# Two-layer product behind a windowed attention: the second layer's stationary tiles are moved by 128 bytes

## The chip, the cores and the metric

The kernel runs on one core of a Trainium2 chip. The metric is the device time of one execution in microseconds, median of the runs shown. The profile is one further execution, seen by the hardware profiler, and its span runs from the first to the last instruction.

## What is computed

An attention over 8 batches, 8 heads, 576 positions and 64 values a head, in which each query sees 32 keys (the last 32 for the first four heads, every fourth of the last 128 for the others), gives 4608 rows of 512 numbers. A two-layer product follows:

```python
h = x @ w_in                       # 4608x512 by 512x2048
g = where(h >= 1, h, where(h <= -1, 0, (h + 1)**2 / 4))
out = g @ w_out                    # 4608x2048 by 2048x512
```

All of it is float32. The weights' words are rebuilt in the kernel from 64-bit input.

## The kernel before

The 4608 rows are cut into 9 tiles of 512 (`TOK`), the 2048 middle columns into 16 chunks of 128 (`NF`), which makes 144 steps (t, f). Each float32 operand of the two layers is split into a high and a low part of type fp32r (`gh` and `gl`, `xh` and `xl`, and two parts of each weight), and a product is the sum of three: high by high, low by high, high by low.

A step of the first layer (`layer1`, L412) is 12 matmuls into one PSUM bank: the stationary operand is a 128x128 block of `wi`, the moving one 128x512 of `xh` or `xl`. The activation of the step follows on VectorE and ScalarE: clamp into a tile `y` (L422), square (L428), maximum with h (L432), high part into `gh` (L439), low part into `gl` (L444). A step of the second layer is again 12 matmuls (L458), with a 128x128 block of `gh` or `gl` stationary and 128x512 of `wo` moving, into four banks that collect over the 16 chunks of a tile:

```python
terms = ((gh, 0), (gl, 0), (gh, 1))
for m, i in order or [(m, i) for m in range(TOK // 128) for i in range(3)]:
    g, w = terms[i]
    PE.matmul(
        out=acc[m],
        lhsT=g[:, 128 * m : 128 * m + 128],
        rhs=weight("wo", f, w, slice(0, DM)),
```

Each matmul is a pair of instructions on TensorE: the load of the stationary block (LDWEIGHTS, PEld in the profile) and the matmul proper. Each second-layer and first-layer matmul has its own load.

The first tile's work is written out by hand in a string of step names (`FIRST`), with the attention of the first eight head pairs and the unpacking of the weights between. From the second tile on a loop sets TensorE's order: `layer1` of step s, then for some steps the scores (L162) or the values (L306) of a later head pair, then `layer2` of step s - 2. So the second layer uses `gh` and `gl` two steps after the first layer has given their h, and in every second step or so some 70 short matmul instructions of the scores or 24 of the values stand between `layer1` and `layer2`. In the last part (from about 705 us) only the two layers are left.

All tiles of SBUF lie in two pools, one after the other along each partition, one place for each tag in the order in which the tags are first asked for. Bytes of a place in each partition, in that order: `small` 2944, `pts` 4608, `qk` 4736, then `wi6`, `wo6`, `wi7`, three buffers of `xh`, `wo7`, three of `xl` (8192 each), `v` 6144, `wi0`, `wi1`, `wo0` (8192), two of `c` (3328), `m0` 4096, `wi2` 8192, `m1` 4096, `wo1`, `wi3`, `wo2`, `wi4`, `wo3`, `wi5`, `wo4` (8192 each), `y` 2048, `gh0`, `gl0`, `gh1`, `gl1`, `gh2`, `gl2` (2048 each), and last `wo5` 8192. The three `gh` and three `gl` places are taken in turn by the steps. Every place after `qk` is a multiple of 256 bytes, so all of `wi`, `wo`, `xh`, `xl`, `y`, `gh` and `gl` start at the same address modulo 256; the places end 384 bytes below the end of the 224 KiB of a partition.

Of the kernel before, what the change touches and what calls it, by code (L numbers as in the profile page):

```python
# [6 lines left out]
F32 = mybir.dt.float32  # L7
F32R = mybir.dt.float32r
# [13 lines left out]
TOK = 512  # L22
NT = B * S // TOK
NF = DF // 128
# [39 lines left out]
def body(ctx, tc, qk, v, v2, mask, w_in, w_out, out):  # L64
# [4 lines left out]
    pool = ctx.enter_context(tc.tile_pool(name="pool", bufs=1))  # L69
# [331 lines left out]
    gs, hps, acc, outs = {}, {}, {}, {}  # L401
# [16 lines left out]
            )  # L418

    def clamped(t, f):  # L420
        gs[t, f] = [pool.tile([128, TOK], F32, tag="y", name=f"y{t}_{f}")]
        nc.vector.tensor_scalar(  # L422
            out=gs[t, f][0], in0=hps[t, f], scalar1=-1.0, scalar2=1.0, op0=ALU.max, op1=ALU.min
        )
# [7 lines left out]
        done.append([nc.vector.tensor_tensor(out=hp, in0=hp, in1=gs[t, f][0], op=ALU.max)])  # L432

    def g_tile(tag, t, f):
        gs[t, f].append(pool.tile([128, TOK], F32R, tag=f"{tag}{(t * NF + f) % 3}", name=f"{tag}{t}_{f}"))
        return gs[t, f][-1]

    def g_high(t, f):
        done[-1].insert(0, nc.scalar.copy(out=g_tile("gh", t, f), in_=hps[t, f]))  # L439

    def g_low(t, f):
        hp = hps.pop((t, f))
        gh = gs[t, f][1]
        nc.vector.tensor_tensor(out=g_tile("gl", t, f), in0=hp, in1=gh.bitcast(F32), op=ALU.subtract)  # L444

    def activation(t, f):
        with tc.high_priority(offset=60):
            for part in (clamped, squared, larger, g_high, g_low):
                part(t, f)
# [83 lines left out]
    def constants_step(count, where):  # L533
# [15 lines left out]
        "E": lambda _, name: block(low_part)(name),  # L549
        "h": products1, "o": products2,  # L550
        "clamp": chunk(clamped), "sq": chunk(squared), "mx": chunk(larger), "gh": chunk(g_high), "gl": chunk(g_low),
    }

# [110 lines left out]
```

## Time and profile before

| what | value |
|---|---|
| time, median of 3 runs | 898.69 us (896.57 to 900.48) |
| span of the profiled execution | 893.7 us; the profile gives no other time of its own |
| TensorE, matmuls | 885.3 us, 99% of the span |
| TensorE, weight loads | 722.2 us, 81% |
| VectorE / ScalarE / GpSimd | 540.3 / 301.3 / 133.2 us |
| second-layer matmuls | 1728 (1152 with `gh`, 576 with `gl`) |
| first-layer matmuls | 1728 |

The median time is 5.0 us above the span. Matmuls overlap one another in the profile: the time of one runs from its start to its modelled end and is longer than the distance to the start of the next, so a pace is read from starts. A timeline row with x2 holds two instructions of one kind, and its start is that of the first.

### The profile page before, as it was taken

To read this page: it belongs to the slowest core of one execution; us is meant where nothing else is said; L and a number is where in the kernel's file an instruction comes from. 1 tells how busy PE (TensorE), PEld (TensorE's weight loads), DVE (VectorE), ACT (ScalarE), POOL (GpSimd) and SP (SyncE) were. 2 spreads that over 40 slices of the span, in tenths; PEclk is the share of its full clock that TensorE was granted. 3 is DMA by queue.
4 is the path that set the end of the run, shared out by engine and by line. 5 is a ranking of instruction groups with operands and counts; after the bars stand their busy time and mean duration, and the time that the engine had idled before them with its cause. 6 is when DMAs were issued, how large, how long until landed. Compare 5 with 4: busy or idle time off the path is not lost.

```text
span 893.7 us, 15852 instructions
## 1 busy us (share of the span) xinstructions
PE 885.3 (99%) x6826; PEld 722.2 (81%) x6826; DVE 540.3 (60%) x854; ACT 301.3 (34%) x508; POOL 133.2 (15%) x84
## 2 busy tenths in 40 slices
PE   8999999999999999999999999999999999999998
PEld 7878878888888888888888888888888888888886
DVE  5898887666666666655665666566665443334333
ACT  3788643232322232232332232223323222222222
POOL 3555441111110101111111110101111000000000
PEclk9999999999999999999999999999999999999999
DMA  9577022101211021102220221101120010001001
GB/s 360 202 299 289 32 64 75 64 28 64 76 50 42 28 66 51 59 29 63 75 64 28 64 75 31 61 28 52 60 63 1 0 48 1 1 1 47 1 1 47
DMA packets 16885, 60.05 MB, mean 67 GB/s; under 512 B 1872, under 2 KB 1872, under 8 KB 14768
## 3 DMA queue, kind: packets, MB, share of 16 engines
q1 hardware_dynamic: 16816, 59.05, 18.8%
q8 instruction: 53, 0.87, 0.4%
q14 instruction: 16, 0.13, 0.1%
HBM read 49.61 MB, written 9.44 MB: 66 GB/s over the span
## 4 chain that ended last, share of the span: by engine, by line
PE 95%; DVE 2%; DMA 1%; issue 1%; ACT 0%; POOL 0%; SPq 0%; POOLq 0%; ACTq 0%
PE acc L458 44%; PE h L412 43%; PE o L306 4%; PE s L162 3%; DMA wi_first<-qk_in 1%; PE consts L146 1%; PE o L296 1%; DVE m_wi L383 0%; DVE m_wo L383 0%; PE t L257 0%; DVE c L204 0%; DVE gl L444 0%; DVE h L432 0%; DVE c L186 0%; POOL c L208 0%
## 5 line engine op out<-in xcount | busy, mean ns | idle before, releaser
L458 PE MATMUL acc<-wo,gh 128*128 128x512 f32 x1152 | 385.1, 395 | 0.0
L412 PE MATMUL h<-xh,wi 128*128 128x512 f32 x1152 | 358.1, 390 | 0.9 <-ACT y L428 0.6
L458 PEld LDWEIGHTS acc<-wo,gh 128*128 128x128 f32 x1152 | 216.2, 188 | 50.8 <-DVE gl L444 0.5
L412 PEld LDWEIGHTS h<-xh,wi 128*128 128x128 f32 x1152 | 216.1, 188 | 47.7 <-DVE gl L444 1.1
L458 PE MATMUL acc<-wo,gl 128*128 128x512 f32 x576 | 224.9, 391 | 0.0
L412 PE MATMUL h<-xl,wi 128*128 128x512 f32 x576 | 224.2, 389 | 0.0
L428 ACT ACTIVATE y<-y,small 128x512 f32<-128x512 f32 x144 | 104.1, 723 | 349.4 <-DVE y L422 348.1
L422 DVE TENSOR_SCALAR y<-h 128x512 f32<-128x512 f32 x144 | 99.1, 688 | 140.7 <-PE h L412 137.4
L432 DVE TENSOR_TENSOR h<-h,y 128x512 f32<-128x512 f32 x144 | 100.5, 698 | 98.7 <-ACT y L428 98.7
L412 PEld LDWEIGHTS h<-xl,wi 128*128 128x128 f32 x576 | 108.1, 188 | 22.2
L458 PEld LDWEIGHTS acc<-wo,gl 128*128 128x128 f32 x576 | 108.2, 188 | 21.1
L444 DVE TENSOR_TENSOR gl<-h,gh 128x512 fp32r<-128x512 f32 x144 | 99.0, 688 | 34.4 <-ACT gh L439 32.6
L439 ACT CAST gh<-h 128x512 fp32r<-128x512 f32 x144 | 84.4, 586 | 100.3 <-DVE h L432 98.0
L208 POOL TENSOR_TENSOR c<-c 96x768 f32<-96x768 f32 x29 | 42.6, 1470 | 444.9 <-DVE c L204 444.8
L241 DVE STREAM_TRANSPOSE pts<-c 32x384 f32<-32x384 f32 x168 | 95.3, 567 | 2.9 <-POOL c L227 0.4
L215 DVE TENSOR_REDUCE c<-c 96x12 f32<-96x768 f32 x30 | 28.4, 947 | 51.1 <-ACT c L212 50.9
L227 POOL TENSOR_TENSOR c<-c 96x768 f32<-96x768 f32 x30 | 44.1, 1471 | 75.5 <-DVE c L223 67.5
L212 ACT ACTIVATE c<-c 96x768 f32<-96x768 f32 x30 | 25.3, 845 | 82.6 <-POOL c L208 74.8
L306 PEld LDWEIGHTS o<-pts,v 128*64 128x64 f32 x672 | 28.6, 137 | 9.9 <-issue 9.5
L306 PE MATMUL o<-pts,v 128*64 128x96 f32 x672 | 33.9, 250 | 0.0
L162 PEld LDWEIGHTS s<-qk 64*32 64x32 f32 x2088 | 23.4, 105 | 10.0 <-issue 9.9
L281 DVE TENSOR_TENSOR xl<-o,xh 128x288 fp32r<-128x288 f32 (+12 forms) x82 | 29.3, 369 | 3.4 <-ACT xh L277 3.3
(72 smaller groups left out, 344.3 us busy)
## 6 DMA issues: line engine op xcount, KB each, us to landing
qk<-qk_in SPq DMA_DIRECT2D x29, 592.0 KB, 3.9
v<-v_in SPq DMA_DIRECT2D x28, 384.0 KB, 3.9
raw_wi<-w_in SPq DMA_DIRECT2D x8, 1024.0 KB, 10.4
raw_wo<-w_in SPq DMA_DIRECT2D x8, 1024.0 KB, 12.3
out<-out SPq DMA_DIRECT2D x32, 256.0 KB, 2.3
wi_first<-qk_in SPq DMA_DIRECT2D x2, 592.0 KB, 6.5
out<-outs SPq DMA_DIRECT2D x4, 256.0 KB, 2.0
wo_first<-qk_in SPq DMA_DIRECT2D x1, 592.0 KB, 8.1
```

Of the source, the lines that this page charges most:

```text
L162: PE.matmul(out=sps[j][QB * g : QB * g + QB, KW * t : KW * t + KW], lhsT=hd["q"][r, QB * b : QB * b + QB], rhs=hd["k"][r, QB * b : QB * b ...
L208: engine.tensor_tensor(out=c, in0=c, in1=spread(n, 0), op=ALU.subtract)
L227: nc.gpsimd.tensor_tensor(out=c, in0=c, in1=spread(n, 2), op=ALU.mult)
L241: nc.vector.transpose(out=pt[r : r + 32, :, 32 * g : 32 * g + 32], in_=c[32 * g : 32 * g + 32, :, 32 * h : 32 * h + 32],)
L306: PE.matmul(out=ops[t // 3][64 * j : 64 * j + 64, 96 * (t % 3) : 96 * (t % 3) + 96], lhsT=hd["v"][:, j, t], rhs=pts[:, j, t], start=True, ...
L412: PE.matmul(out=hp, lhsT=weight("wi", f, w, slice(128 * c, 128 * c + 128)), rhs=xtile(t)[x][:, c], start=start and (c, w, x) == terms[0], ...
L422: nc.vector.tensor_scalar(out=gs[t, f][0], in0=hps[t, f], scalar1=-1.0, scalar2=1.0, op0=ALU.max, op1=ALU.min)
L428: nc.scalar.activation(out=y, in_=y, func=AF.Square, bias=half_t, scale=0.5)
L432: done.append([nc.vector.tensor_tensor(out=hp, in0=hp, in1=gs[t, f][0], op=ALU.max)])
L439: done[-1].insert(0, nc.scalar.copy(out=g_tile("gh", t, f), in_=hps[t, f]))
L444: nc.vector.tensor_tensor(out=g_tile("gl", t, f), in0=hp, in1=gh.bitcast(F32), op=ALU.subtract)
L458: PE.matmul(out=acc[m], lhsT=g[:, 128 * m : 128 * m + 128], rhs=weight("wo", f, w, slice(0, DM)), start=f == 0 and i == 0, stop=f == NF - ...
```

## The change

The place of `y` is made 128 bytes longer (32 unused floats), and that of `gl2`, the last of the six stationary places, likewise. So `gh0` to `gl2` start 128 bytes further on, and `wo5`, which lies behind them, 256 bytes further on. Nothing else moves: the tiles that are used, the instructions and their order are as before.

```diff
     def clamped(t, f):
-        gs[t, f] = [pool.tile([128, TOK], F32, tag="y", name=f"y{t}_{f}")]
+        gs[t, f] = [pool.tile([128, TOK + 32], F32, tag="y", name=f"y{t}_{f}")[:, :TOK]]
...
     def g_tile(tag, t, f):
-        gs[t, f].append(pool.tile([128, TOK], F32R, tag=f"{tag}{(t * NF + f) % 3}", name=f"{tag}{t}_{f}"))
+        n = (t * NF + f) % 3
+        pad = 32 if (tag, n) == ("gl", 2) else 0
+        g = pool.tile([128, TOK + pad], F32R, tag=f"{tag}{n}", name=f"{tag}{t}_{f}")
+        gs[t, f].append(g[:, :TOK])
         return gs[t, f][-1]
```

## Rows read from the trace of the kernel before

**Rows 1.** The page: busy time, share of the span and instructions of each engine.
```profile
PE 885.3 (99%) x6826; PEld 722.2 (81%) x6826; DVE 540.3 (60%) x854; ACT 301.3 (34%) x508; POOL 133.2 (15%) x84
```
**Rows 2.** The page: the chain that ended last, by engine and by line.
```profile
PE 95%; DVE 2%; DMA 1%; issue 1%; ACT 0%; POOL 0%; SPq 0%; POOLq 0%; ACTq 0%
PE acc L458 44%; PE h L412 43%; PE o L306 4%; PE s L162 3%; DMA wi_first<-qk_in 1%; PE consts L146 1%; PE o L296 1%; DVE m_wi L383 0%; DVE m_wo L383 0%; PE t L257 0%; DVE c L204 0%; DVE gl L444 0%; DVE h L432 0%; DVE c L186 0%; POOL c L208 0%
```
**Rows 3.** The page: costliest groups; busy us, mean ns of one, idle before.
```profile
L458 PE MATMUL acc<-wo,gh 128*128 128x512 f32 x1152 | 385.1, 395 | 0.0
L412 PE MATMUL h<-xh,wi 128*128 128x512 f32 x1152 | 358.1, 390 | 0.9 <-ACT y L428 0.6
...
L458 PE MATMUL acc<-wo,gl 128*128 128x512 f32 x576 | 224.9, 391 | 0.0
L412 PE MATMUL h<-xl,wi 128*128 128x512 f32 x576 | 224.2, 389 | 0.0
```
**Rows 4.** The chain in order of time, 520 to 560 us: start, us, what.
```profile
522.39 2.72 PE h L412 x12
525.11 0.90 PE s L162 x69
526.01 2.96 PE acc L458 x12
528.97 2.72 PE h L412 x12
531.69 1.14 PE o L306 x24
532.83 2.99 PE acc L458 x12
535.82 2.72 PE h L412 x12
538.54 2.72 PE acc L458 x12
```
**Rows 5.** Timeline, all engines, 750 to 756 us, the two layers alone: start, us, what.
```profile
750.68 0.19 PEld L458 LDWEIGHTS acc<-wo,gh 128*128 128x128 f32 x1
750.90 0.39 PE L458 MATMUL acc<-wo,gh 128*128 128x512 f32 x1
750.91 0.19 PEld L458 LDWEIGHTS acc<-wo,gl 128*128 128x128 f32 x1
751.11 0.69 DVE L422 TENSOR_SCALAR y<-h 128x512 f32<-128x512 f32 x1 [1.80 <-PE h L412]
751.13 0.39 PE L458 MATMUL acc<-wo,gl 128*128 128x512 f32 x1
...
753.62 0.62 PE L412 MATMUL h<-xh,wi 128*128 128x512 f32 x2
...
754.05 0.69 DVE L444 TENSOR_TENSOR gl<-h,gh 128x512 fp32r<-128x512 f32 x1 [0.71 <-ACT gh L439]
```
**Rows 6.** Busy time by stretch: length, engines (x instructions), granted clock, DMA share, GB/s.
```profile
532.76:535.43 2.67, 2.67 (x13) 2.17 (x12) 2.10 (x6) 1.33 (x5) 1.45 (x1) 1.00 0.18 69
...
750.90:753.62 2.72, 2.72 (x13) 2.25 (x12) 1.39 (x2) 0.91 (x2) 0.00 (x0) 1.00 0.00 0
```
**Rows 7.** Timeline of TensorE's matmuls after the values of a pair, 531.9 to 537.5 us.
```profile
531.62 1.21 PE L306 MATMUL o<-pts,v 128*64 128x96 f32 x24
532.76 0.50 PE L458 MATMUL acc<-wo,gh 128*128 128x512 f32 x1
533.11 0.40 PE L458 MATMUL acc<-wo,gl 128*128 128x512 f32 x1
533.35 0.63 PE L458 MATMUL acc<-wo,gh 128*128 128x512 f32 x2
533.81 0.40 PE L458 MATMUL acc<-wo,gl 128*128 128x512 f32 x1
534.05 0.62 PE L458 MATMUL acc<-wo,gh 128*128 128x512 f32 x2
534.50 0.40 PE L458 MATMUL acc<-wo,gl 128*128 128x512 f32 x1
534.74 0.62 PE L458 MATMUL acc<-wo,gh 128*128 128x512 f32 x2
535.20 0.39 PE L458 MATMUL acc<-wo,gl 128*128 128x512 f32 x1
535.43 0.39 PE L458 MATMUL acc<-wo,gh 128*128 128x512 f32 x1
535.66 0.62 PE L412 MATMUL h<-xh,wi 128*128 128x512 f32 x2
```
**Rows 8.** Timeline of TensorE's weight loads at the same break, 532.3 to 534.5 us.
```profile
532.76 0.19 PEld L458 LDWEIGHTS acc<-wo,gh 128*128 128x128 f32 x1
532.87 0.19 PEld L458 LDWEIGHTS acc<-wo,gl 128*128 128x128 f32 x1
533.11 0.43 PEld L458 LDWEIGHTS acc<-wo,gh 128*128 128x128 f32 x2
```
**Rows 9.** Groups by line and shape, weight loads: busy us, mean ns, idle before.
```profile
L458 PEld LDWEIGHTS acc<-wo,gh 128*128 128x128 f32 x1152 | 216.2, 188 | 50.8 <-DVE gl L444 0.5
L306 PEld LDWEIGHTS o<-pts,v 128*64 128x64 f32 x672 | 28.6, 137 | 9.9 <-issue 9.5 <-DVE c L204 0.4
```
**Rows 10.** Groups by line and shape, matmuls of the values: busy us, mean ns, idle before.
```profile
L306 PE MATMUL o<-pts,v 128*64 128x96 f32 x672 | 33.9, 250 | 0.0
```

## The prediction

> **What bounds the kernel now.** I read the page first: the busy times say that TensorE's matmuls fill 99% of the span while no other engine is above 60% [rows 1]. That alone proves little, since overlapping matmuls make a busy engine. The chain that ended last settles it: 95% of the span is TensorE, 44% the second layer's line and 43% the first layer's [rows 2], and the groups of both lines have at most 0.9 us of idle time before them [rows 3]. So the end is set by how closely one matmul follows another, and the change can act on nothing else. The reader should next see the chain in order of time: a group of 12 matmuls takes 2.72 us in either layer, unless short matmuls of the attention stand before it; then the group lasts 2.96 or 2.99 us [rows 4].
>
> The timeline gives the pace. Where only the two layers are left, 12 second-layer matmuls start between 750.90 and 753.62 us [rows 5]: 2.72 us / 12 = 226.7 ns each, at a granted clock of 1.00 [rows 6], which is the level of 2.4 GHz. 226.7 ns are 544 clocks for 512 columns. At a column per clock 213.3 ns would do, so each matmul spends 13.3 ns, 32 clocks, on something. The weight load of the next matmul begins 0.01 us after each matmul [rows 5], so it runs beside the stream of the moving operand. How long it reads is seen at a break: the first two loads stand 532.76 and 532.87 us, 0.11 us apart, and the third waits for its matmul [rows 8]. So it is over before half of the 226.7 ns, and nothing waits for it to end; if it costs the running matmul time, it does so by being in its way.
>
> **The trace speaks for such a thing.** After the values of a head pair, the spacings of the second layer are not 0.227 us but, from 533.11 us on, 0.24, 0.23 (mean of two), 0.24, 0.225, 0.24, 0.23, 0.23, 0.23 [rows 7]: 11 matmuls from 533.11 to 535.66 us, 231.8 ns each, with no wait of an engine between them, after which 226.7 ns returns. The same instructions on the same tiles at the same clock take different times, in a pattern that dies away. That looks like two streams that settle into step with each other. The two that run together are the weight load and the moving operand, and in this kernel both always start at one address modulo 256. No row shows the other case; that is the open quantity of this prediction.
>
> **The change, part by part.** It adds and removes no instruction, no wait and no transfer; the order on each engine and queue stays. By the widths in the list of places, `y` becomes 2176 bytes, 8.5 times 256, so the six stationary places lie 128 bytes off every other tile modulo 256; `gl2`, 2176 bytes too, brings `wo5` back to its old remainder. 256 of the 384 free bytes are used. The first layer's operands don't move at all: it is the control.
>
> *VectorE and ScalarE* write `gh` and `gl` at new addresses. If that changed their 0.69 us [rows 5], the cover is large: the clamp of a step starts at 751.11 and its `gl` is done at 754.05 + 0.69 = 754.74 us [rows 5], while the second layer reads it two steps later, at 750.90 + 2 x 5.44 = 761.78 us. 7 us of slack; I cost it at nothing. The bank of h is wanted again at 750.90 + 5.44 + 2.72 = 759.06 us, 4.3 us after `gl` let go of it, so a faster TensorE meets no wait there either, and VectorE at 540.3 us [rows 1] is no bound.
>
> *The pace of the second layer* is the whole of it: 1152 + 576 = 1728 matmuls [rows 3]. Below, the bound is a column per clock: 13.3 ns x 1728 = 23.0 us less. Above, the bound is the longest single spacing after a break, 0.24 us [rows 7]: 13.3 ns x 1728 = 23.0 us more. For the value I take a matmul whose load doesn't disturb it. The nearest row is that of the values, with smaller loads (64 columns, 137 ns against 188 ns [rows 9]): 24 instructions of 96 columns fill 1.21 us [rows 7], the last of them 0.25 us [rows 10], so 23 spacings take 0.96 us, 41.7 ns each, 1.7 ns above the 40.0 ns of 96 columns. With the same 1.7 ns, 512 columns take 215.0 ns, 11.7 ns less than now: 11.7 x 1728 = 20.2 us less. That it can be had at all rests on the mechanism above, not on a row.
>
> The Trainium skill, TensorE: Matmul & The Clock Gate, section Back-to-back issue gap, gives an isolated matmul of 512 columns about N / 2.4 + 2.5 ns, or 216 ns; by that estimate the sum would be (226.7 - 215.8) x 1728 = 18.8 us less, close to mine. This trace has no second-layer spacing that short.
>
> *What is late next.* If the two streams fall into step, they may have to do so again wherever the relation changes, that is at the start of each of the 144 groups of the first layer. A full settling costs 11 x (231.8 - 226.7) = 56 ns [rows 7]; 144 of them are 8.1 us more, none is nothing. I take half, 4.0 us, because the first layer follows without a pause, while the settling seen follows a break. The settling that the second layer now pays after some 46 breaks (scores and values of the 23 pairs that the loop begins with the scores) would go: 46 x 0.056 = 2.6 us less at most; I take half, 1.3 us.
>
> **The sum.** -20.2 + 4.0 - 1.3 = -17.5 us, against the profiled execution: a span of 893.7 us becomes 876.2. The median lies 5.0 us above the span, so 898.7 - 17.5 = **881 us** (2% faster).
>
> **The rivals.** *No effect: the load is not in the way.* Then the 32 clocks belong to the matmul itself, and 898.7 us stays. For it: the steady 226.7 ns is the same in both layers to the last digit, as a fixed cost would be, and the disturbance after a break could be something that needs a pause and no neighbour. Against it: a fixed cost doesn't swing from 0.225 to 0.24 us between like instructions [rows 7]. The Trainium skill speaks for this rival: on the same page, section Step-by-step: what each phase is for, TensorE has two independent read ports, and loading the next weights takes no read bandwidth from the running matmul. To it I also count the case that the streams do meet but with another period than 256 bytes, and that of a small gain given back: 5 ns less in each second-layer matmul (8.6 us) and a full settling in the first layer (8.1 us) leave 898 us. Together 0.25.
>
> *Slower: the new offset is the worse of the two.* If the cost depends on which part of a 256-byte stretch each stream is in, the present relation may be the good one, and the second layer would stay at what it shows out of step: 231.8 ns, 5.1 x 1728 = 8.8 us more, 907.5 us; at most 0.24 us, 921.7 us. For it: after each break the pattern settles toward the present spacing, so this is a state that the two streams seek. Against it: 32 lost clocks in each matmul is already a large cost for a good relation, and 0.225 us is seen once in passing. It decides as soon as the second layer's mean spacing is above 226.7 + 4.5 / 1.728 = 229.3 ns. 0.20.
>
> *The tiles don't lie where the change says.* If places were rounded up to 256 bytes or taken in another order, nothing would move and 898.7 us would stay. The order of first use puts the seven places side by side and the padding is what the list adds up, so I give it no more than 0.02, within the 0.25.
>
> **How the numbers follow.** Faster by the mechanism: 0.55, with a range of its own from 875.7 (a column per clock) to 891 (half of the 17.5 us and a little more lost). No effect: 0.25. Slower: 0.20. Half a per cent, 4.5 us, is about what a measurement of this kernel can tell from no change. A range of 8 in 10 must take in the first two cases, with the runs' own spread of 2 us either way, and the mildest of the third: 875 to 905 us. What is left out is the greater part of the slower case, above 905 us, and a gain at its very bound.
>
> **What the profile after would show.** Right: groups of 12 on the second layer's line take about 2.58 us in the chain (12 x 215.0 ns) where nothing precedes them, those of the first layer 2.72 to 2.78 us, and the second layer's share of the chain falls below the first's. The load after a break still needs its 0.11 us. The settling term is right if the first spacings of each first-layer group are uneven, wrong if they are 226.7 ns from the first on. No effect: 2.72 us in both layers and the same pattern after breaks. Slower: second-layer groups of 2.78 us or more with nothing before them. A change of the first layer's steady pace, or a wait of TensorE for VectorE, would show that I have the wrong engine or the wrong cause. The forecast rests on one inference, from an unsteady spacing to two reading streams; if that is wrong, everything but the control is wrong.

## The result and the profile after

The changed kernel takes 908.48 us (median of 5 runs, 906.64 to 910.48) against 898.69 us (5 runs, 895.31 to 900.48): a ratio of the means of 1.011, 95% interval 1.008 to 1.014. It is 1.1% slower, where 881 us and a gain of 2% were forecast; the time is outside the stated range, and 1 us from the rival that called the new offset the worse of the two (907.5 us). The profiled execution has a span of 904.9 us, 11.2 us more than before. Each run's own span lies some 1.8 us below its time (here 906.64 and 904.9 us), so the 5.0 us of the prediction was mostly the runs' spread; both profiled executions are among the short ones, and the 11.2 us compare like with like.

The page after shows first the chain that ended last, by engine and by line, then the two layers' groups (busy us, mean ns of one, idle before). The second layer's line is now L461:

```profile
PE 98%; DVE 1%; issue 1%; ACT 0%; ACTq 0%
PE acc L461 45%; PE h L412 43%; PE o L306 4%; PE s L162 3%; PE consts L146 1%; PE o L296 1%; PE s L146 1%; DVE m_wi L383 0%; PE t L257 0%; DVE y L422 0%; DVE h L432 0%; ACT gh L442 0%; DVE c L186 0%; ACT wo L390 0%; ACT y L428 0%
...
L461 PE MATMUL acc<-wo,gh 128*128 128x512 f32 x1152 | 389.9, 399 | 0.0
L412 PE MATMUL h<-xh,wi 128*128 128x512 f32 x1152 | 359.7, 391 | 0.6 <-ACT y L428 0.6
...
L461 PE MATMUL acc<-wo,gl 128*128 128x512 f32 x576 | 227.2, 394 | 0.0
L412 PE MATMUL h<-xl,wi 128*128 128x512 f32 x576 | 225.5, 392 | 0.0
```

Beside [rows 3], the second layer's two groups have grown by 4.8 and 2.3 us, together 7.1 us, and the first layer's, whose operands were not moved, by 1.6 and 1.3 us, together 2.9 us. These 10.0 us of the 11.2 are the loss, and sums of the spacings from start to start give the same 7.1 and 2.9. No idle time came with them: TensorE still waits for nobody, it is slower while it works. By the same spacings, the second layer lost 6.8 us in its groups with no break before them (1092 matmuls, 6.2 ns each) and 0.1 us in the groups behind a break (600 matmuls).

The chain in order of time (start, us, what), around the last break for the attention:

```profile
708.01 1.14 PE o L306 x24
709.15 2.98 PE acc L461 x12
712.13 2.73 PE h L412 x12
714.86 2.80 PE acc L461 x12
717.66 2.76 PE h L412 x12
```

The reader is to see three things beside [rows 4]. A group of the second layer with nothing before it takes 2.80 us, not 2.72. A group of the first layer that follows one of these takes 2.76 us. And after a break little is new: 2.98 us stands where 2.96 and 2.99 stood, and the first-layer group behind it is back at 2.73.

The timeline of TensorE's matmuls between two such groups:

```profile
714.70 0.40 PE L461 MATMUL acc<-wo,gh 128*128 128x512 f32 x1
714.94 0.40 PE L461 MATMUL acc<-wo,gl 128*128 128x512 f32 x1
715.17 0.62 PE L461 MATMUL acc<-wo,gh 128*128 128x512 f32 x2
...
717.49 0.62 PE L412 MATMUL h<-xh,wi 128*128 128x512 f32 x2
```

From 714.70 to 717.49 us 12 matmuls start, 232.5 ns each, and the spacings never become even as in [rows 5]. To the nanosecond, worked out from the starts in the trace, this group runs 241, 232, 231, 232, 228, 230, 233, 241, 232, 231, 232, 233: a pattern of seven that begins again. The first-layer group behind it runs 236, 224, 231, 236, 228, 232, 231 and then 227 ns, which by the starts are the numbers of the kernel before after a break (a stretch of [rows 7]); its last one, beside which the second layer's first block is loaded, is 232 ns again. So the second layer no longer settles, and the first layer has to settle behind it, except behind a group that itself follows a break: there it starts even (2.73 us).

### The profile page after: what moved, and what is told of

Same layout as the page of the kernel before. It is cut to its first block, busy times and chain, and to the rows that moved or that the text cites. A ratio compares the mean times of both kernels' runs of the same rounds, so it can differ in the third digit from the quotient of the medians.

```text
span 904.9 us, 15852 instructions
## 1 busy us (share of the span) xinstructions
PE 896.1 (99%) x6826; PEld 723.7 (80%) x6826; DVE 540.3 (60%) x854; ACT 301.7 (33%) x508; POOL 133.4 (15%) x84
## 4 chain that ended last, share of the span: by engine, by line
PE 98%; DVE 1%; issue 1%; ACT 0%; ACTq 0%
PE acc L461 45%; PE h L412 43%; PE o L306 4%; PE s L162 3%; PE consts L146 1%; PE o L296 1%; PE s L146 1%; DVE m_wi L383 0%; PE t L257 0%; DVE y L422 0%; DVE h L432 0%; ACT gh L442 0%; DVE c L186 0%; ACT wo L390 0%; ACT y L428 0%
## 5 line engine op out<-in xcount | busy, mean ns | idle before, releaser
L461 PE MATMUL acc<-wo,gh 128*128 128x512 f32 x1152 | 389.9, 399 | 0.0
L461 PEld LDWEIGHTS acc<-wo,gh 128*128 128x128 f32 x1152 | 216.9, 188 | 54.2 <-DVE gl L447 0.5
L461 PE MATMUL acc<-wo,gl 128*128 128x512 f32 x576 | 227.2, 394 | 0.0
L461 PEld LDWEIGHTS acc<-wo,gl 128*128 128x128 f32 x576 | 108.6, 189 | 23.0
L162 PEld LDWEIGHTS s<-qk 64*32 64x32 f32 x2088 | 23.8, 107 | 10.1 <-issue 9.8
```

The source lines that it names most:

```text
L162: PE.matmul(out=sps[j][QB * g : QB * g + QB, KW * t : KW * t + KW], lhsT=hd["q"][r, QB * b : QB * b + QB], rhs=hd["k"][r, QB * b : QB * b ...
L461: PE.matmul(out=acc[m], lhsT=g[:, 128 * m : 128 * m + 128], rhs=weight("wo", f, w, slice(0, DM)), start=f == 0 and i == 0, stop=f == NF - ...
```

## The experiments

The theory of the prediction had two parts: the distance of the two operands modulo 256 bytes sets the spacing, and it does so because the weight load that runs beside a matmul is in the way of its moving stream, which costs the 32 clocks above a column per clock. The runs test the parts separately. Beside the first three kernels the kernel before ran again and took 896.70 us (median of 19 runs), beside the two last of this section 897.85 us (median of 12; one more, of 3102 us, is left out). The ratios are of means against these runs, the spans against 893.7 us.

**A whole period.** The place of `y` is 256 bytes longer, that of `gl2` as before:

```diff
-        gs[t, f] = [pool.tile([128, TOK + 32], F32, tag="y", name=f"y{t}_{f}")[:, :TOK]]
+        gs[t, f] = [pool.tile([128, TOK + 64], F32, tag="y", name=f"y{t}_{f}")[:, :TOK]]
...
-        pad = 32 if (tag, n) == ("gl", 2) else 0
+        pad = 0 if (tag, n) == ("gl", 2) else 0
```

> The stationary places are moved by 256 bytes instead of 128 (the place of y is 256 bytes longer, that of gl2 as before the change). Theory (distance modulo 256): the time of before, 898.7 us, span about 894, every steady group of 12 matmuls 2.72 us. Rival (any displacement of these places, or a longer place of y, costs the 10 us): about 908 us.

896.63 us, ratio 1.001 (0.999 to 1.003), span 894.1 us. In its chain every late group is back at

```profile
707.94 2.72 PE acc L461 x12
710.66 2.72 PE h L412 x12
```

Displacing the tiles, or a longer place of `y`, costs nothing by itself.

**Both operands moved.** An earlier place is 128 bytes longer, which moves all tiles of both layers alike:

```diff
-    small = const.tile([128, 9 * KW + 96 + 64], F32, name="small")
+    small = const.tile([128, 9 * KW + 96 + 96], F32, name="small")
```

> Every tile from the second place of SBUF on is moved by 128 bytes, so all operands of both layers lie at another remainder modulo 256 but at the old distance from each other. Theory (only the distance counts): 898.7 us, 2.72 us a group in both layers. Rival (the remainder of the stationary place itself counts): 2.80 us a group in the second layer and the same in the first, so about 908 to 918 us.

895.83 us, ratio 1.000 (0.998 to 1.001), span 894.0 us, 2.72 us in every late group of its chain. The remainder of the stationary place itself doesn't count; its distance to the moving one does.

**A quarter.** The distance is 64 bytes:

```diff
-        gs[t, f] = [pool.tile([128, TOK + 32], F32, tag="y", name=f"y{t}_{f}")[:, :TOK]]
+        gs[t, f] = [pool.tile([128, TOK + 16], F32, tag="y", name=f"y{t}_{f}")[:, :TOK]]
...
-        pad = 32 if (tag, n) == ("gl", 2) else 0
+        pad = 48 if (tag, n) == ("gl", 2) else 0
```

> The stationary places of the second layer are moved by 64 bytes instead of 128, the last weight tile back to its old remainder. Theory (distance modulo 256, with the cost set by how the two streams fall into step): a time that differs from both kernels is possible; between a column per clock in the second layer (876 us) and the 233 ns of distance 128 (908 us), I expect about 903, an unsteady spacing in the second layer and an uneven start of the first. Rival (only one bit of the address, that of 128 bytes, counts): 898.7 us as at distance 0, since 64 bytes leave half of each stretch of 128 where it was, or half of the loss, 903.6 us.

910.01 us, ratio 1.015 (1.012 to 1.017), span 904.8 us. The size was missed: 64 bytes cost as much as 128. Its chain:

```profile
715.00 2.80 PE acc L461 x12
717.80 2.75 PE h L412 x12
```

Here the spacings alternate, 236 and 231 ns by the starts, mean 233.3. That falls against a rule of one address bit: at 64 bytes it gave no loss or half of it.

**The spacing by itself.** A kernel of nothing but series of 48 equal matmuls on two tiles at one remainder modulo 256:

```python
for i, (name, so, sc, mo, mc) in enumerate(SERIES):
    p = ps.tile([128, 512], F32, tag=f"b{i % 8}", name=name)
    for _ in range(REPEAT):
        PE.matmul(out=p[:sc, :mc], lhsT=w[:, so : so + sc], rhs=x[:, mo : mo + mc], start=True, stop=True)
```

> A kernel that leaves out the whole computation and runs only series of 48 fp32r matmuls each, each matmul with its own weight load, 128 columns stationary and 512 moving, back to back. In 16 series the stationary block starts 0, 16, 32 to 240 bytes after the moving one, modulo 256; further series have distances of 256 and 384 bytes, both operands moved by 128 bytes or the moving one alone, 64 and 32 stationary columns, and 384 and 256 moving columns. Theory (the weight load and the moving stream meet in SBUF, and the cost hangs on their distance modulo 256): about 226.7 ns each at distance 0 and at 256, about 233 ns on average and unsteady at 128 and 384, 226.7 ns with both moved by 128 bytes; other distances lie somewhere between 213.3 and 241 ns; with 64 or 32 stationary columns the cost above 213.3 ns shrinks with the columns (13.3 to about 7 and 3 ns), and with 256 moving columns it is as large as with 512, 13 ns above 106.7 ns. First rival (the cost belongs to the matmul and only a place that is no multiple of 256 bytes from the pool's start disturbs it): both operands moved by 128 bytes are as slow as one moved. Second rival (something else in the kernel, such as VectorE or ScalarE writing the moved tiles, slows the second layer): 226.7 ns in every series of 128 by 512, since no other engine works here.

In its timeline each row is a series; the difference of two starts over 48 is the mean spacing. `db`, `dc` and `dd` have distances of 16, 32 and 48 bytes; `fa` has the moving operand alone moved by 128 bytes, `fb` both; `ga` has 64 stationary columns, `gc` 32, both at distance 0; `ha` and `hb` have fewer moving columns:

```profile
18.07 11.05 PE L45 MATMUL db<-x,w 128*128 128x512 f32 x48
28.95 11.35 PE L45 MATMUL dc<-x,w 128*128 128x512 f32 x48
40.15 11.36 PE L45 MATMUL dd<-x,w 128*128 128x512 f32 x48
...
207.06 11.30 PE L45 MATMUL fa<-x,w 128*128 128x512 f32 x48
218.20 11.04 PE L45 MATMUL fb<-x,w 128*128 128x512 f32 x48
229.08 11.20 PE L45 MATMUL ga<-x,w 128*64 128x512 f32 x48
240.12 11.26 PE L45 MATMUL gb<-x,w 128*64 128x512 f32 x48
251.21 11.28 PE L45 MATMUL gc<-x,w 128*32 128x512 f32 x48
262.33 8.51 PE L45 MATMUL ha<-x,w 128*128 128x384 f32 x48
270.68 5.91 PE L45 MATMUL hb<-x,w 128*128 128x256 f32 x48
276.43 5.85 PE L45 MATMUL hc<-x,w 128*128 128x256 f32 x48
```

At 16 bytes 10.88 us / 48 = 226.7 ns, at 32 bytes 11.20 / 48 = 233.3; by the starts of rows not shown, 227.1 at 240 bytes (the first spacings settle), 226.9 at 256 and 232.5 at 384. With the moving operand alone moved 232.1, with both 226.7. All distances from 32 to 224 bytes lie between 228.9 and 234.4 ns in their last 24 spacings; none is under 226.7. So the period of 256 bytes and the distance are shown without any other engine at work, and for 512 columns no distance of this scan is better than that of the kernel before. For 256 columns it is otherwise: `hc`, at 128 bytes, takes 118.7 ns in its last 24 spacings, and `hb`, at distance 0, 120.0.

The second part of the theory misses here. With 64 and 32 stationary columns, whose loads take 134 and 108 ns in place of 188, the spacing is not smaller but 230.0 and 231.7 ns; it doesn't settle, so this alone doesn't tell what the load costs. With 384 and 256 moving columns the spacing is 174.0 and 119.8 ns, once settled 173.3 and 120.0. So 128 columns more cost 53.3 ns each time, a column per clock at the granted clock of 1.00, and 13.3 ns stay above it (160.0 and 106.7): a fixed price for each matmul. The theory forecast that too, since each matmul still has a full load beside it.

**Which of the two blocks, and which stream.** The same kernel with other series: offsets in turn, finer distances, operands read from one address again and again, bf16:

```python
if kind in "sb":
    left = w[:, 0:1].broadcast_to([128, 128])
if kind in "mb":
    right = x[:, 0:1].broadcast_to([128, 512])
```

> A kernel that leaves out the whole computation and runs only series of 48 matmuls of 128 stationary and 512 moving columns with a weight load each. Each matmul k has its own stationary block, loaded before it starts, and beside it the block of matmul k + 1 is loaded. In one series the offsets alternate so that a matmul's own block is always 128 bytes off its moving operand while the block loaded beside it is at distance 0; in another its own block is at distance 0 and the one loaded beside it 128 bytes off. Theory (the load that runs beside a matmul meets its moving stream): the first of these settles at 226.7 ns, the second is unsteady at about 232 ns. Rival (a matmul is slow when its own block lies elsewhere): the other way round. Further series: distances of 4, 8, 12, 244 and 252 bytes (theory: near distance 0 nothing changes, 226.7 ns, or at the ends of that stretch up to 233 ns); stationary, moving, or both operands read from one and the same address again and again, so that one stream or both don't walk through SBUF (theory: if the 32 clocks above a column per clock come from the meeting of two walks, they shrink towards 215 ns; rival, a fixed cost of a matmul or of its load: 226.7 ns in all three); bf16 operands at distances 0, 64 and 128 bytes (theory: half the bytes, so less than 226.7 ns, near 216 ns, and less or no difference between the distances).

Timeline rows of its series: `kb` and `kc` alternate the offsets, `kd` only that of the moving operand, `na`, `nb` and `nc` are bf16 at distances 0, 128 and 64, `pb` reads the moving operand from one address, `pc` both operands:

```profile
18.09 11.20 PE L64 MATMUL kb<-x,w 128*128 128x512 f32 x48
29.13 11.14 PE L64 MATMUL kc<-x,w 128*128 128x512 f32 x48
40.11 11.20 PE L64 MATMUL kd<-x,w 128*128 128x512 f32 x48
...
128.56 10.53 PE L64 MATMUL na<-xh,wh 128*128 128x512 bf16 x48
138.93 10.52 PE L64 MATMUL nb<-xh,wh 128*128 128x512 bf16 x48
149.28 10.52 PE L64 MATMUL nc<-xh,wh 128*128 128x512 bf16 x48
...
170.76 10.66 PE L64 MATMUL pb<-x,w 128*128 128x512 f32 x48
181.26 10.66 PE L64 MATMUL pc<-x,w 128*128 128x512 f32 x48
```

With the moving operand at one address the spacing falls to 10.50 us / 48 = 218.8 ns; with the stationary block at one address it doesn't fall (231.7 ns in its last 24 spacings, after a first one of 417). bf16 takes 216.0 ns and the same at distance 128 (215.6); its loads are shorter too, 98 ns, so it separates nothing by itself. The first of these says that 8 of the 13.3 ns, more than half of the 32 clocks, go when the moving operand no longer walks through SBUF, while the load beside it walks as before. The alternating series decide nothing: 230.0 ns for `kb` and 228.8 for `kc`, neither the 226.7 of one theory nor the 232 of the other, and by 1 ns the rival's way round. Perhaps a moving operand that jumps by 128 bytes at each matmul unsettles the train by itself; `kd`, where only it alternates, takes 230.0, but there the distances alternate as well, so this is not shown. Distances of 4, 8, 12 and 244 bytes gave 232.5, 230.7, 230.0 and 233.3 ns by the starts, 252 bytes 226.7; the stretch of good distances is ragged.

**No load beside.** Groups that stand apart, so that the last matmul of a group has no load beside it; VectorE reads its result as soon as it is done:

```python
for _ in range(groups):
    for k in range(group):
        PE.matmul(out=p[:, :cols], lhsT=a[:, so : so + 128], rhs=right, start=True, stop=True)
    nc.vector.tensor_scalar(
        out=a[:, so : so + 2], in0=p[:, cols - 2 : cols], scalar1=0.0, scalar2=0.5, op0=ALU.mult, op1=ALU.add
    )
```

> A kernel that leaves out the whole computation and runs groups of matmuls (128 by 512, a load each) that stand apart: after the last matmul of a group VectorE reads its result and writes a column pair of the stationary block, and the next group's first load waits for that. So the last matmul of a group has no weight load beside it. What is read is the time from its start to VectorE's start, for groups of 12, of 2 and of 1, at distances 0, 64 and 128 bytes, with the moving operand read from one address, and with bf16 operands. In the kernel before, VectorE's clamp starts 0.426 us after the last first-layer matmul of a group, whether a load runs beside that matmul or not. Theory as predicted (the load beside the matmul costs it 32 clocks and more at distance 128): without a load the time is the same at distances 0, 64 and 128 and about 0.413 us, 13 ns shorter than 0.426. Rival (the 32 clocks belong to the walk of a 4-byte moving operand and not to the load): 0.426 us at distance 0 without any load, some 8 ns less with the moving operand at one address, 10 to 11 ns less with bf16. If the distance then still matters without a load beside, the cost comes from where a matmul's own block was read, or from the state that earlier matmuls leave, and not from a meeting of two reads.

The matmuls of different series ran mixed in this run, so that in most groups a load of another series followed at once; it decides nothing. The same with a fixed order:

> As the run before, with the series kept in their written order (there they were mixed, so that a bf16 load ran beside the last matmul of most groups), and groups of 12 and of 3. The computation is again left out as a whole. Read is the time from the start of a group's last matmul, which has no load beside it, to VectorE's start. Theory as predicted (the load beside a matmul costs it 32 clocks, more at distance 128): about 0.413 us for every distance, against 0.426 us with a load. Rival (the 32 clocks belong to the walk of a 4-byte moving operand, and the distance acts without a load beside): 0.426 us at distance 0, 8 ns less with the moving operand at one address, 11 ns less with bf16, and at 64 and 128 bytes 0.426 to 0.44 us by the state in which the group has arrived there.

Its timeline at the end of a group at distance 0 and of one with the moving operand at one address. The first row of a pair holds the last two matmuls, the second VectorE's read:

```profile
40.69 0.61 PE L57 MATMUL ga<-x,w 128*128 128x512 f32 x2
41.34 0.16 DVE L58 TENSOR_SCALAR w<-ga 128x2 fp32r<-128x2 f32 x1 [3.11 <-PE ga L57]
```

```profile
157.96 0.60 PE L57 MATMUL gd<-x,w 128*128 128x512 f32 x2
...
158.60 0.16 DVE L58 TENSOR_SCALAR w<-gd 128x2 fp32r<-128x2 f32 x1 [2.98 <-PE gd L57]
```

From the start of the last matmul to VectorE's start, worked out from the trace: 426 ns at distance 0 in groups of 12, 418 with the moving operand at one address, 417 with bf16. The kernel before has the same pair without any experiment: where a break follows, the next load starts some 317 ns after the last first-layer matmul, and the clamp starts 426 ns after it (24 groups after 100 us); where the second layer's load runs beside, 427 (82 groups). So a matmul without a load beside it is not 13 ns shorter, the 8 ns of the moving operand's walk show without a load too, and the rival of this run stands; bf16 came out 9 ns shorter, not 11. At distances of 64 and 128 bytes the last matmul takes 425 to 428 or 433 to 436 ns, and so it does at distance 0 in groups of 3, which have not settled: its length follows the state in which the train is, not its own distance.

**One block off.** A settled train at distance 0 in which every 24th matmul differs:

```python
odd = k % 24 == 23
PE.matmul(
    out=p[: sc if odd else 128],
    lhsT=w[:, so : so + sc] if odd else w[:, :128],
    rhs=x[:, mo : mo + 512] if odd else x[:, :512],
    start=True, stop=True,
)
```

> A kernel that leaves out the whole computation and runs series of 168 back-to-back fp32r matmuls at distance 0, in which every 24th matmul alone differs: its stationary block lies 128, 64, 32, 192 or 256 bytes off modulo 256, or has 64 columns, or its moving operand lies 128 bytes off, or both do. Before each of these the train has settled at 226.7 ns. Call the odd one k. Its load runs beside matmul k - 1, whose own block and moving operand are as always. If the load that runs beside a matmul acts on it, the spacing after k - 1 departs from 226.7 ns first (to about 232 ns at 128 bytes, as at the last first-layer matmul before each second-layer group of the changed kernel), and at 256 bytes nothing departs. If a matmul's own block counts instead, the spacing after k - 1 stays and that after k departs. In both cases the settling that follows should last some ten matmuls, as after a break.

Spacings in ns after the matmuls k - 2, k - 1, k (the odd one), k + 1 and so on, worked out from the starts in the trace:

```
                             k-2  k-1    k  k+1  k+2  k+3  k+4
block 256 bytes off          227  227  226  227  227  226  227
block 128 bytes off          226  233  234  227  226  227  227
block 64 bytes off           226  227  235  229  232  231  227
block 32 bytes off           226  236  228  233  230  227  227
block 64 columns wide        226  226  236  229  231  232  227
moving operand 128 off       226  227  234  226  226  227  227
block and moving both off    225  234  231  234  230  234  236
```

At 128 and 32 bytes the spacing after k - 1 departs at once: matmul k - 1 has its usual block and its usual moving operand, and only the load that runs beside it reads elsewhere. So the load beside acts at once, by 6 to 10 ns. At 64 and 192 bytes, or with a narrower block, matmul k - 1 is left alone and the disturbance shows one matmul later. A single odd block costs 13 to 20 ns in all and is over after one to four matmuls, where some ten were expected; jumping with both operands costs 60 ns and the whole settling of some eleven matmuls.

The changed kernel itself shows that it is the running matmul that gets longer, and not only the start of the next that comes late. Its first layer lies at distance 0, and what differs is the load beside the last matmul of a group: none before a break (first pair of rows), the second layer's block, 128 bytes off, where no break follows (second pair):

```profile
707.63 0.39 PE L412 MATMUL h<-xl,wi 128*128 128x512 f32 x1
...
708.05 0.69 DVE L422 TENSOR_SCALAR y<-h 128x512 f32<-128x512 f32 x1 [1.91 <-PE h L412]
...
714.47 0.40 PE L412 MATMUL h<-xl,wi 128*128 128x512 f32 x1
...
714.90 0.69 DVE L422 TENSOR_SCALAR y<-h 128x512 f32<-128x512 f32 x1 [2.67 <-PE h L412]
```

By the starts after 100 us, VectorE reads the result 425 ns (24 groups) and 433 ns (82 groups) after the matmul's start, against 426 and 427 in the kernel before. With the load 64 bytes off, in the run of the quarter, it is 426, as the table says.

**The other layer.** In the kernel before, the first layer's moving tiles 128 bytes off, by 32 floats more in the places `wi7` and `v`:

```diff
+        if tag == "wi7":
+            return pool.tile([128, 4 * TOK + 32], dt, tag=tag, name=name)[:, : 4 * TOK].rearrange("p (a b) -> p a b", a=4)
         return pool.tile([128, 4, TOK], dt, tag=tag, name=name, bufs=bufs)
...
-            both = pool.tile([128, 1536], F32, tag="v", name=f"v{n}")
+            both = pool.tile([128, 1536 + 32], F32, tag="v", name=f"v{n}")[:, :1536]
```

> The kernel before, with the first layer's moving tiles (xh, xl) 128 bytes off its stationary tiles modulo 256 instead of the second layer's; as a side effect the last weight tile of the second layer (chunks 14 and 15, 18 of 144 steps) is 128 bytes off too. Theory: steady groups of the first layer take 2.80 us and those of the second, which now follow an unsteady stretch and have to settle, 2.76 us, where no attention stands before them. First layer 144 x 0.08 = 11.5 us, second layer about 98 x 0.04 = 3.9 us, so a span of about 908.5 and a time of about 912 us, more than the change under study because the breaks stand before the second layer and no break resets the first. Rival (something particular to the second layer's tiles, written by VectorE and ScalarE just before use): 898.7 us.

906.88 us, ratio 1.010 (1.007 to 1.013), span 906.1 us. Where the second layer's weights are not the moved ones, its chain (first layer L414, second L460) reads

```profile
733.50 2.73 PE acc L460 x12
736.23 2.79 PE h L414 x12
```

The layers have changed parts: the first doesn't settle, the second settles anew each time, within three spacings (232, 233, 230 ns). The forecast of 912 us was too high: by the starts the first layer lost 10.1 us, not 11.5, and the second 0.7, not 3.9, since its settling is 0.01 us a group, not 0.04.

**One eighth of the weights.** Only the padding behind `gl2` stays, so that `wo5` alone (chunks 10 and 11) is off:

```diff
-        gs[t, f] = [pool.tile([128, TOK + 32], F32, tag="y", name=f"y{t}_{f}")[:, :TOK]]
+        gs[t, f] = [pool.tile([128, TOK], F32, tag="y", name=f"y{t}_{f}")[:, :TOK]]
```

> Only the padding behind gl2 is made, that of y is not: so one of the eight weight tiles of the second layer, which serves chunks 10 and 11 (18 of 144 steps), lies 128 bytes off the stationary tiles, all else is as before. Theory: 2.80 us in the second-layer groups of those two chunks and about 2.76 us in the first-layer group that follows each, 18 x (0.08 + 0.04) = 2.2 us less what breaks hide, so a span of about 895.5 and a time of about 900.5 us; all other groups 2.72 us. Rival (the place of the stationary tiles or of y is what counts): 898.7 us and 2.72 us everywhere.

899.62 us, ratio 1.001 (0.999 to 1.003): the 2 us can't be told in the time. The chain tells them:

```profile
782.46 2.79 PE acc L461 x12
785.25 2.73 PE h L412 x12
787.99 2.79 PE acc L461 x12
790.78 2.74 PE h L412 x12
793.52 2.72 PE acc L461 x12
```

Two groups of 16 are slow, and their neighbours hardly (2.73 and 2.74 us, where 2.76 was forecast); by the starts the two layers together lost 1.4 us of the forecast 2.2. The span of this execution, 898.3 us, is no measure of it: by the starts, 3 us of it lie in the spacings after TensorE's short matmuls, most of them early, where TensorE's granted clock was 1.00 up to 20 us and 0.83 from there to 40 us, against 0.91 and 1.00 in the kernel before.

No version of these beats the kernel before; the scan, at 512 columns, has no distance that would.

## Why the prediction was wrong, by its own steps

*What bounds the kernel* was right: TensorE's pace alone, 98% of the chain, and no wait came into the two layers. *The parts costed at nothing* were right too; VectorE is at 540.3 us as before.

*The step that failed is the reading of the 13.3 ns.* The prediction took the 32 clocks above a column per clock for what a weight load costs the matmul beside it, and so expected a load at another place to give them back. The runs show them without a load (426 ns to VectorE, 427 with one), and no smaller with a shorter load (230.0 ns) or one from a single address (231.7 ns); they shrink to 13 clocks (218.8 ns) when the moving operand stops walking, and to 6 with bf16 (216.0 ns). The clean 215.0 ns was thus not to be had at any distance tried. Its source was misread too: by the starts in the trace the values' short matmuls come in pairs, 7 and then 76 ns apart, so 41.7 ns is a mean of two unlike spacings and no price of a matmul with an undisturbed load. In place of the 215.0 ns stands 2.80 us / 12 = 233 ns: the term of -20.2 us was in fact +7.1.

*The sign of the unevenness* was read the wrong way for the same reason. That the pattern after a break dies away [rows 7] was read as two streams that settle, and the runs bear out that the load beside can act on a matmul (233 in place of 227 ns at once). But what they settle into at distance 0 is the good state, and the new distance has none that is as good. The second rival said this, with its place and price: 231.8 ns and 907.5 us, against 232.5 to 233 ns and 908.5 us. That its time came within 1 us is partly luck: it charged 5.1 ns to all 1728 matmuls and nothing to the first layer, while the trace has 6.2 ns in 1092 of them, next to nothing in the groups behind breaks, and 2.9 us in the first layer. The evidence for it stood in the same rows as the forecast's, and deserved more than 0.20: a pattern that ends in a steady spacing speaks for the present relation, while nothing in the trace spoke for another.

*What is late next* was right in kind and sized well: the first layer settles anew, though not behind the second layer's groups that follow a break; 0 to 8.1 us forecast, 4.0 taken, 2.9 measured. *The settling saved after breaks* did not come: 2.98 us stands beside 2.96 and 2.99, and the groups behind breaks gained nothing in place of -1.3 us.

The Trainium skill's rule that the load takes no read bandwidth from the running matmul (TensorE: Matmul & The Clock Gate, section Step-by-step: what each phase is for) agrees with the first finding and not with the second: with a load 128 bytes off, the running matmul took 233 ns in place of 227, and the measurement decides. Its N / 2.4 + 2.5 ns (section Back-to-back issue gap) is met by bf16, 216.0 ns, and by no fp32r series here.

*What stays open.* That the distance modulo 256 decides is shown; how it does is not. The load beside is not the whole of it: in the run with a fixed order, last matmuls without any load took up to 436 ns where the train had not settled, at distance 0 too. Nor is the distance: at 128 bytes the spacings alternate 238 and 229 ns in one series of the scan (`di`) and run the pattern of seven of the changed kernel in a series with the same offsets in the next run (`qb`), so what went before counts too. Why 0, 16, 240 and 252 bytes settle at 226.7 ns and 4 to 12 or 244 bytes do not, and why a block 64 bytes off leaves the matmul beside it alone and slows the next, no run here explains. Where the 5 ns that stay with the moving operand at one address come from is open too. Some 1.1 us of the 11.2 us of span lie outside the two layers' lines; 0.7 us of them is one wait of the first scores (3.0 us in place of 2.3), which is 2.9 us in the run with both operands moved as well, so it is no work of the change.

## What to carry to other kernels

A steady spacing above a column per clock is not yet a conflict that a new address would remove: first find out whether the excess stays when the suspected neighbour is absent; here the last matmul before each break gave that answer in the trace before. If fp32r operands are used, and 512 columns move, lay the stationary and the moving tile at the same address modulo 256 bytes, and check tile widths for paddings that break it; for 256 columns measure first, since there 128 bytes cost nothing. A pattern that dies away after a disturbance says that the present arrangement has a steady state, and a change that may remove it is a risk before it is a chance.

## What the runs showed of the hardware

- The spacing of fp32r matmuls (128 by 512) depends on the distance between stationary and moving operand modulo 256 bytes: 226.7 ns at 0, 16, 240, 252 and 256 bytes, 229 to 234 ns at the others tried. bf16 shows no such thing: 216 ns at distances 0 and 128. Nor do 256 columns at 128 bytes: 118.7 ns, against 120.0 at distance 0.
- An fp32r matmul at distance 0 costs a fixed 13.3 ns above a column per clock at 256, 384 and 512 columns; at 512 it keeps them without a load beside it (426 ns to the reader of its result, 427 with one); with a load of fewer columns the spacing is longer (230.0 ns with 64 columns, 231.7 with 32), not shorter.
- A load of a block 128 bytes off lengthens the fp32r matmul that it runs beside: its result is read 433 ns after its start, not 426, and the next starts 233 ns after it, not 227. One 64 bytes off does neither.
- A train of matmuls has a memory of some ten matmuls: after a break, a jump of both operands, or an uneven group, the same spacings come in the same order (236, 224, 231, 236, 228, 233, 231 ns) before it is even again.
